# A real-input transform's first step: sums and differences of mirrored rows, five columns of the index grid per product

## The chip, the cores and the metric

One core of a Trainium2 chip. The time is device time of one execution in microseconds (us), lower is better. All runs in this document were in the fast state (granted clock 0.996 to 0.999), so all may be compared. "Before" and "after" are the kernel without and with the change; the variants are named e1 to e10.

## The reference

Eight sequences of 3008 tokens and 256 channels go through a Fourier filter, then all 24064 tokens through a SwiGLU block. Cut to what matters:

```python
x: (8, 3008, 256)   filt_r, filt_i: (1505, 256)   w_gate, w_val: (256, 1536)   w_out: (1536, 256)
X = np.fft.rfft(x, axis=1)
y = np.fft.irfft(X * (filt_r + 1j * filt_i), n=3008, axis=1)
t = y.reshape(24064, 256)
out = (silu(t @ w_gate) * (t @ w_val)) @ w_out
```

## The kernel before

The transform of 3008 = 47 x 64 points is made of short products: the first step transforms along n1 (47 rows, N1) for each of the 64 values of n2. As the input is real, 24 results s (NS), each with a real and an imaginary part, are enough. While TensorE works on the SwiGLU block of batch b, which is the bulk of the time, pieces of the transform of batch b+1 are put between its instructions, by a fixed order (the generators below are advanced at marked places of it). Each `yield` ends a piece. `pin` keeps the order of an engine's instructions as written.

The tables of the first step (both parities h of the row number share one product, so the matrix has two blocks with zeros beside them, 94 by 96):

```python
NR = 2 * N1            # 94
NK = 4 * NS            # 96
NV = 2
N_ONE = 32 // NV       # 16 first steps a batch
...
    w = np.stack([np.cos(ph), -np.sin(ph)], 1)
    wf = np.zeros((N1, 2, NS, 2, 2))
    ...
    for h in range(2):
        wf[:, h, :, :, h] = w.transpose(0, 2, 1)
```

The loads, and the step itself: one product, one copy out of PSUM, one store by ScalarE to a DRAM buffer (d1) that the second step reads back in another order:

```python
            elif u < N_ONE:
                self.x[u] = xpool.tile([NR, NV, C], FP32, name=f"x_{self.b}_{u}", tag="x")
                rows = x[self.b].rearrange("(r n) c -> r n c", n=32)

                for r in (slice(0, 80), slice(80, NR)):
                    self.load(out=self.x[u][r], in_=rows[r, ts(u, NV), :])
...
        def stage1(self, u):

            t1 = t1pool.tile([NK, NV, C], FP32, name=f"t1_{self.b}_{u}", tag="t1", bufs=2)
            ps = self.bank(f"pa_{self.b}_{u}")
            pin(nc.tensor.matmul(out=ps[0:NK], lhsT=wf_t, rhs=self.x.pop(u),
                                         start=True, stop=True))
            self.load_x(u + 2)
            yield
            pin(nc.scalar.copy(out=t1, in_=ps[0:NK]))
            pin(nc.scalar.dma_start(out=self.d1_rows[:, ts(u, NV), :], in_=t1))
```

`self.load` issues on the sync queue; `xpool` has two buffers.

Of the kernel before, what the change touches and what calls it, by code (L numbers as in the profile page):

```python
# [41 lines left out]
FP32 = mybir.dt.float32  # L42
U32 = mybir.dt.uint32
# [5 lines left out]
B, S, C = 8, 3008, 256  # L49
# [4 lines left out]
N1, N2 = 47, 64  # L54
NS, NQ = 24, 64
# [14 lines left out]
NV = 2  # L70
N_ONE = 32 // NV
N_TWO = NS // NV


WO = {1: 0, 7: 1, 2: 2, 3: 3, 5: 4, 6: 5, 4: 6}
# [46 lines left out]
def dft_tables():  # L122
    n1, n2 = np.arange(N1), np.arange(N2)
    s, q = np.arange(NS), np.arange(NQ)
    ph = 2 * np.pi * (np.outer(n1, s) % N1) / N1
    w = np.stack([np.cos(ph), -np.sin(ph)], 1)
    wf = np.zeros((N1, 2, NS, 2, 2))
    wi = np.zeros((NS, 2, 2, N1, 2))

    v = np.stack([2 * np.cos(ph), -2 * np.sin(ph)], 0)  # L130
    v[0, :, 0], v[1, :, 0] = 1.0, 0.0
    for h in range(2):
        wf[:, h, :, :, h] = w.transpose(0, 2, 1)
        wi[:, :, h, :, h] = v.transpose(2, 0, 1) / S
    one = wi[:, :, 0, :, 0].transpose(1, 0, 2).reshape(2 * NS, N1)
    back = np.zeros((128, 10 * N1))
    for tile_, first in zip(BACK, BACK_AT):
        for i, (_, row, a, rows) in enumerate(tile_):
            back[row:row + rows, first + N1 * i:first + N1 * (i + 1)] = one[a:a + rows]


    kap = np.where(q[:, None] < 32, s + N1 * q[:, None], s + N1 * (95 - q[:, None]))
    sg = np.where(q < 32, 1.0, -1.0)[:, None]
    th = 2 * np.pi * ((n2[:, None, None] * kap) % S) / S
    c, sn = np.cos(th), np.sin(th)
    d = np.zeros((2, N2, NS, 2, NQ))
    d[0, :, :, 0] = c.transpose(0, 2, 1)
    d[1, :, :, 0] = sn.transpose(0, 2, 1)
    d[0, :, :, 1] = (-sn * sg).transpose(0, 2, 1)
    d[1, :, :, 1] = (c * sg).transpose(0, 2, 1)  # L150
    d = d.reshape(128, NS, 128)
    de = np.stack([d, d.transpose(2, 1, 0)], 2)

    pairs = np.arange(128).reshape(2, N2).T.ravel()
    later = np.stack([de[:, :, 0], de[:, :, 1][:, :, pairs]], 2)
    f32 = np.float32
    return (wf.reshape(NR, NK).astype(f32), wi.reshape(NK, NR).astype(f32),
            back.astype(f32), np.ascontiguousarray(de).astype(f32),
            np.ascontiguousarray(later).astype(f32))


# [1 line left out]
def kernel(  # L163
# [8 lines left out]
    out: bass.AP,  # L172
):
    nc = tc.nc
    wf_host, wi_host, back_host, de_host, later_host = dft_tables()
    wf_dram = nc.inline_tensor(wf_host, name="wf_tbl")
    wi_dram = nc.inline_tensor(wi_host, name="wi_tbl")
    back_dram = nc.inline_tensor(back_host, name="back_tbl")
    de_dram = nc.inline_tensor(de_host, name="de_tbl").ap()
    later_dram = nc.inline_tensor(later_host, name="later_tbl").ap()  # L180
# [7 lines left out]
    xpool = pool("xp", 2)  # L188
    t1pool = pool("t1", 2)
# [36 lines left out]
    one = cpool.tile([128, 1], FP32)  # L226
# [15 lines left out]
    pin = tc.keep_in_program_order  # L242

    def add(eng, dst, a, b):
        return eng.tensor_tensor(out=dst, in0=a, in1=b, op=ALU.add)  # L245

    def sub(eng, dst, a, b):
        return eng.tensor_tensor(out=dst, in0=a, in1=b, op=ALU.subtract)  # L248
# [221 lines left out]
    preparation = Preparation()  # L470
    TICKS = 20

    back_t = []

    def load_back():

        t = rpool.tile([128, 2, 128, 2], U32, name="back", tag="raw", bufs=2)
        t = t.bitcast(FP32).rearrange("p b f two -> p (b f two)")
        back_t.append(t[:, 0:10 * N1])
        pin(nc.sync.dma_start(out=back_t[0], in_=back_dram.ap()))  # L480
# [6 lines left out]
    def fbank(name):  # L487
        return fps.tile([128, NV, C], FP32, name=name, tag="f")
# [7 lines left out]
    class Spectral:  # L496
# [25 lines left out]
        def load_x(self, u):  # L522
            if self.b == 0:
                rows = x[0].rearrange("(r n) c -> r n c", n=32)
                for a, n in ((0, 4), (4, 4)):
                    for r in (slice(0, 80), slice(80, NR)):
                        self.load(out=x0[u][r, a:a + n, :],
                                  in_=rows[r, 8 * u + a:8 * u + a + n, :])
            elif u < N_ONE:
                self.x[u] = xpool.tile([NR, NV, C], FP32, name=f"x_{self.b}_{u}", tag="x")  # L530
                rows = x[self.b].rearrange("(r n) c -> r n c", n=32)

                for r in (slice(0, 80), slice(80, NR)):
                    self.load(out=self.x[u][r], in_=rows[r, ts(u, NV), :])

        def load_two(self, u):
            if u < N_TWO:
                self.tb[u] = lend("tb", u).rearrange("p i (k c) -> p i k c", k=2)
# [41 lines left out]
        def bank(self, name):  # L580

            if self.b == 0:
                return bank(name).rearrange("p (i c) -> p i c", i=NV)
            return fbank(name)

        def stage1(self, u):

# [21 lines left out]
        def turn(self, u):  # L609

            if u >= N_TWO:
                return
# [9 lines left out]
        def stage2a(self, u):  # L622
# [24 lines left out]
            yield  # L647
            pin(add(nc.vector if self.b == 0 and u == N_TWO - 1 else nc.gpsimd, pt, pt, qt))

        def real_part(self, u):  # L650

            if u < N_TWO and u % 3:
                self.real[u] = early("fr", u)
# [233 lines left out]
    rpool = pool("raw", 1)  # L887
# [11 lines left out]
    with tc.tile_pool(name="start", bufs=1) as spool0:  # L899
# [12 lines left out]
        n = 0  # L912
        while n < NPR - 1:
            pair = ORDER[n][0] in "ABE" and ORDER[n + 1][0] in "ABE"
# [32 lines left out]
        for u in range(N_TWO + lag):  # L947
            if u < N_TWO:
                spec.turn(u + 2)
                step = spec.stage2a(u)  # L950
# [32 lines left out]
        following = Spectral(1)  # L983
# [78 lines left out]
    for b in range(B):  # L1062
        cur, nxt = spec, following if b + 1 < B else None
        spec, following = nxt, Spectral(b + 2)
# [3 lines left out]
            return [s.stage3(k, step) for step in range(4)]  # L1068

        d = [three(cur, k) for k in range(1, NCHUNK)]  # L1070
        one = [nxt.stage1(u) for u in range(N_ONE)] if nxt else []
        two = []
        for u in range(N_TWO + 2) if nxt else ():
            two += [nxt.stage2b(u - 2)] if u > 1 else []
# [21 lines left out]
        for step in range(NCHUNK * NG + (b == B - 1)):  # L1096
            ghost = step == NCHUNK * NG
            k, g = order_of(b)[min(step, NCHUNK * NG - 1)]
            this = None
            pieces = []  # L1100
            if not ghost:
                pieces = plan[step]
                this = Group(b, k, g, cur.y[k], sequence_of(cur, nxt, step))
                if b == 0:
                    preparation.finish(step)
                chunk = {0: 1, 2: 2, 5: 3}.get(step)
                if b and chunk:
                    cur.load_t4(chunk, 0)
            elif before is None:
                break  # L1110
            ends = {ORDER[e - 1]: n for n, (_, e) in enumerate(PIECES)}
            last = ghost or b == B - 1 and step == NCHUNK * NG - 1
            for place, token in enumerate(SCHEDULE):
                if b == 0 and this and place * TICKS % len(SCHEDULE) < TICKS and \
                        (step or place > SCHEDULE.index("A01")):
                    preparation.tick(step)
                old = token.endswith("'")
                op = token.rstrip("'")
                if op[0] == "t":
                    n = int(op[1])  # L1120
                    ps = pieces_before if old else pieces
                    if n < len(ps):
                        next(ps[n], None)
                elif op[0] in "Wo" or op.endswith(".o"):

                    g0 = older if old else before
                    if g0 is not None and (old or not ghost):
                        g0.project(op)
                else:
                    g0 = before if old else this  # L1130
                    if g0 is not None and not (ghost and op[0] == "S"):
                        g0.step(op)
                if old or this is None:
                    continue
                if nxt and (step, op) == ((4, "P2") if b else (5, "A23")):
                    nxt.load_two(0)
                if b + 2 < B and (step, op) == (9, "B01"):
                    for u in range(2):
                        following.load_x(u)
                if b and chunk and op == "B01":  # L1140
                    cur.load_t4(chunk, 1)
                for i in range(2):
                    if nxt and (step, op) == (10, ("A12", "E23")[i] if b else "E23"):
                        nxt.load_t4(0, i)
                for f, args in chores.get((step, op), ()) if b == 0 else ():
                    f(*args)
                if op in ends and not last and (b or step >= NT * NG - 1):
                    reload_weights((g + 1) % NG, ends[op])
            older, before, pieces_before = before, this, pieces
# [33 lines left out]
```

## Time and profile before

| | before |
|---|---|
| median of 3 runs at first, range | 2941.1 us (2937.6 to 2943.2) |
| span of the profiled run | 2935.5 us |
| TensorE, VectorE, ScalarE, GpSimd busy | 99%, 66%, 55%, 54% |
| chain of work that ended last | TensorE 94% |
| first steps: matmul, copy | 112 of each in batches 1 to 7, 0.86 us of TensorE each |

The kernel is bound by TensorE nearly everywhere. So a change pays what it takes off TensorE, less the waits that it gives TensorE. Such waits are short (mostly 0.1 to 1 us) and begin behind other instructions, so the totals by engine hardly show them. What shows them is the chain, the timeline, and a comparison of the two traces matmul by matmul.

### The profile page before, as it was taken

How to read it: one execution, taken by the hardware profiler on the slowest of the kernel's cores; microseconds unless marked ns; L12 is line 12 of the kernel's file. 1: busy time of each engine (PE TensorE's matmuls, PEld its weight loads, DVE VectorE, ACT ScalarE, POOL GpSimd, SP SyncE). 2: the span in 40 equal slices, each digit the busy share in tenths (PEclk: the TensorE clock that was granted, in tenths of full speed). 3: DMA queues.
4: the chain of work that ended last, by engine and by line, in shares of the span. 5: the costliest groups of instructions: out<-in, count | busy, mean ns of one | idle time of the engine just before them, and what ended most of it. 6: DMA issues, size and time to landing. Idle time of an engine off the chain costs nothing.

```text
span 2935.5 us, 57365 instructions
## 1 busy us (share of the span) xinstructions
PE 2901.7 (99%) x20040; PEld 2805.6 (96%) x20040; DVE 1927.4 (66%) x4384; ACT 1609.7 (55%) x4208; POOL 1579.9 (54%) x1759
## 2 busy tenths in 40 slices
PE   7999999999999999999999999999999999999999
PEld 5889999999999999999999999999999999999999
DVE  6888765576655676557765667656666566666665
ACT  6775455555555555555455554555555555555554
POOL 3876655556444655456554556454564545555453
PEclk9999999999999999999999999999999999999999
DMA  8677855575555755556646566556665566644442
GB/s 227 213 258 250 304 189 179 179 229 180 179 182 186 223 186 166 189 183 205 213 155 193 184 203 211 164 177 203 194 199 173 177 208 194 200 139 154 148 130 88
DMA packets 225661, 558.82 MB, mean 190 GB/s; under 512 B 32666, under 2 KB 110474, under 8 KB 225374
## 3 DMA queue, kind: packets, MB, share of 16 engines
q1 hardware_dynamic: 190286, 485.84, 52.6%
q10 hardware_dynamic: 26160, 45.43, 4.3%
q0 software_dynamic: 8928, 23.89, 2.3%
q8 instruction: 161, 2.64, 0.4%
q14 instruction: 126, 1.03, 0.1%
HBM read 459.97 MB, written 95.05 MB: 189 GB/s over the span
## 4 chain that ended last, share of the span: by engine, by line
PE 94%; DVE 1%; POOL 1%; ACT 0%; issue 0%; DVEq 0%; POOLq 0%
PE wa L791 24%; PE wA L870 17%; PE wk L791 16%; PE we L791 12%; PE wG L870 9%; PE wF L870 4%; PE pa L590 3%; PE pd L696 3%; PE pc L662 2%; PE pb L630 2%; PE pd L699 0%; POOL y_t L245 0%; DVE h L838 0%; POOL wt_t L245 0%; POOL wt_t L248 0%
## 5 line engine op out<-in xcount | busy, mean ns | idle before, releaser
L791 PE MATMUL wa<-y_t,wt_t 128*128 128x188 f32 x4464 | 878.8, 323 | 3.8 <-issue 1.4
L791 PEld LDWEIGHTS wa<-y_t,wt_t 128*128 128x128 f32 x4464 | 730.2, 190 | 28.6 <-issue 17.3
L245 POOL TENSOR_TENSOR h<-h 128x376 f32<-128x376 f32 x190 | 182.8, 983 | 779.2 <-DVE h L838 779.2
L870 PE MATMUL wA<-wo_t,h 128*128 128x128 f32 x4608 | 576.9, 275 | 2.3 <-DVE o L245 1.7
L870 PEld LDWEIGHTS wA<-wo_t,h 128*128 128x128 f32 x4608 | 563.0, 192 | 16.3 <-issue 10.8
L791 PE MATMUL wk<-y,wt_t 128*128 128x188 f32 x2976 | 566.2, 323 | 0.0
L248 POOL TENSOR_TENSOR h<-h 128x376 f32<-128x376 f32 x570 | 554.8, 995 | 0.5
L791 PEld LDWEIGHTS wk<-y,wt_t 128*128 128x128 f32 x2976 | 479.1, 190 | 25.9 <-issue 19.8
L248 DVE TENSOR_TENSOR we<-we,m 128x376 f32<-128x376 f32 x576 | 318.4, 556 | 195.2 <-PE we L791 134.1
L791 PE MATMUL we<-y_t,wt_t 128*128 128x188 f32 x2232 | 431.5, 323 | 1.4 <-ACT we L822 1.4
L791 PEld LDWEIGHTS we<-y_t,wt_t 128*128 128x128 f32 x2232 | 369.4, 190 | 1.8 <-ACT we L822 1.7
L248 POOL TENSOR_TENSOR D<-f,f 128x376 f32<-128x376 f32 x288 | 280.7, 988 | 103.3 <-ACT f L806 102.6
L252 DVE SCALAR_TENSOR_TENSOR y<-wk,c 128x376 f32<-128x376 f32 x480 | 244.8, 542 | 131.4 <-ACT we L822 55.0
L826 ACT COPY m<-wa 128x376 f32<-128x376 f32 x576 | 272.0, 472 | 87.1 <-PE wa L791 85.9
L833 ACT ACTIVATE g<-wa 128x188 f32<-128x188 f32 x576 | 187.9, 326 | 187.5 <-PE wa L791 180.0
L870 PE MATMUL wG<-wo_t,h 128*128 128x128 f32 x2304 | 288.3, 275 | 0.6 <-DVE o L245 0.6
L870 PEld LDWEIGHTS wG<-wo_t,h 128*128 128x128 f32 x2304 | 281.4, 192 | 0.8 <-DVE o L245 0.8
L833 ACT ACTIVATE u<-we 128x188 f32<-128x188 f32 x576 | 188.9, 328 | 168.2 <-DVE we L248 149.9
L806 ACT ACTIVATE f<-wk 128x376 f32<-128x376 f32 x288 | 139.4, 484 | 234.4 <-PE wk L791 213.2
L810 ACT COPY c<-wk 128x376 f32<-128x376 f32 x288 | 136.0, 472 | 226.1 <-PE wk L791 226.1
L813 DVE SCALAR_TENSOR_TENSOR x<-wk,f 128x376 f32<-128x376 f32 x192 | 104.3, 543 | 234.4 <-PE wk L791 228.6
L822 ACT COPY we<-y 128x376 f32<-128x376 f32 x480 | 224.1, 487 | 32.9 <-DVE h L838 14.2
(144 smaller groups left out, 3893.8 us busy)
## 6 DMA issues: line engine op xcount, KB each, us to landing
wt_t<-w_all SPq DMA_DIRECT2D x174, 896.0 KB
wt_t<-w_all SPq DMA_DIRECT2D x174, 768.0 KB
d<-t ACTq DMA_DIRECT2D x112, 192.0 KB
lent<-later_tbl SPq DMA_DIRECT2D x84, 256.0 KB
lent<-in_filt_r_dram SPq DMA_DIRECT2D x336, 64.0 KB
lent<-d SPq DMA_DIRECT2D x84, 256.0 KB
d<-lent ACTq DMA_DIRECT2D x84, 256.0 KB
x<-in_x_dram SPq DMA_DIRECT2D x112, 160.0 KB
```

The costliest lines, as they stand in the source:

```text
L245: return eng.tensor_tensor(out=dst, in0=a, in1=b, op=ALU.add)
L248: return eng.tensor_tensor(out=dst, in0=a, in1=b, op=ALU.subtract)
L252: return nc.vector.scalar_tensor_tensor(out=dst, in0=a, scalar=-1.0, in1=b, op0=ALU.mult, op1=ALU.subtract)
L590: pin(nc.tensor.matmul(out=ps[0:NK], lhsT=wf_t, rhs=self.x.pop(u), start=True, stop=True))
L791: pin(nc.tensor.matmul(out=ps[:, z], lhsT=self.wt[:, SLOT[p], z], rhs=rhs, start=start and z == 0, stop=True, skip_group_check=True))
L806: pin(act.mul(self.small(f"f{i}", f"f{i}", 1), t[f"k{i}"], -1.0))
L810: pin(act.copy(out=self.small(f"c{i}", f"c{i}", 1), in_=t[f"k{i}"]))
L813: pin(v.scalar_tensor_tensor(out=dst, in0=t[f"k{j}"], scalar=-1.0, in1=t[f"f{i}" if j == 3 else f"D{at}"], op0=ALU.mult, op1=ALU.add))
L822: pin(act.copy(out=self.bank(f"e{at}"), in_=t[f"y{at}"]))
L826: pin(act.copy(out=self.small(f"m{at}", "m", 4), in_=t[f"a{at}"]))
L833: pin(act.activation(out=self.small(op, "g", 3, 1)[:, 0], in_=ps[:, 1], func=AF.Silu))
L870: pin(nc.tensor.matmul(out=self.tiles[at][:, t, :], lhsT=self.hs[i][:, HID[p], t0:t0 + 128], rhs=wo_t[:, JB * q + i, WO[p], :], start=star ...
```

## The change

In the first step's table, w[n1] holds the factors by which row n1 is multiplied, and w[47 - n1] is the conjugate of w[n1]. So the real part needs only the sums x[n1] + x[47 - n1], the imaginary part only the differences, and each contraction falls from 47 rows to 24 (with row 0) and 23. Then five n2 fit into one product of 120 by 120, and two products with 256 columns each make five n2, where one with 512 columns made four. That is 13 steps a batch for 16. The price: VectorE makes the sums and differences (for step u+1, one piece after step u), and five n2 in one tile make loads and stores of x and of the result a pattern of three dimensions. Batches 2 to 7 are changed; 0 and 1 stay. The diff, with tables and declarations cut:

```diff
@@ dft_tables
+    paired = np.zeros((NP * (NPAIR + 1), 2, NS, NP))          # NP = 5, NPAIR = 23
+    for j in range(NP):
+        paired[NPAIR * j:NPAIR * (j + 1), :, :, j] = w[1:NPAIR + 1]
+        paired[NP * NPAIR + j, 0, :, j] = 1.0
 ... (declarations, and the load of the table once)
@@ load_x
+            elif self.b > 1:
+                if u < N_PAIRED:                              # 13
+                    t = xpool.tile([NP * (NPAIR + 1), 2, C], FP32, name=f"x_{self.b}_{u}", tag="x")
+                    n2, pairs = min(NP * u, N2 - NP), NP * NPAIR
+                    rows = x[self.b].rearrange("(n1 n2) c -> n2 n1 c", n2=N2)
+                    back = bass.AP(tensor=x.tensor,
+                                   offset=x.offset + ((self.b * N1 + N1 - 1) * N2 + n2) * C,
+                                   ap=[[C, NP], [-N2 * C, NPAIR], [1, C]])
+                    self.load(out=t[0:pairs, 0], in_=rows[n2:n2 + NP, 1:NPAIR + 1])
+                    self.load(out=t[0:pairs, 1], in_=back)
+                    self.load(out=t[pairs:pairs + NP, 0], in_=rows[n2:n2 + NP, 0])
+                    self.x[u] = t
@@ stage 1
+        def pair(self, u):
+
+            if u < N_PAIRED:
+                a, b = [self.x[u][0:NP * NPAIR, i] for i in range(2)]
+                pin(sub(nc.vector, differences[u % 2], a, b))
+                pin(add(nc.vector, a, a, b))
+
+        def stage1_paired(self, u):
+
+            t1 = t1pool.tile([NP * NS, 2, C], FP32, name=f"t1_{self.b}_{u}", tag="t1", bufs=2)
+            ps = self.bank(f"pa_{self.b}_{u}")[0:NP * NS]
+            table = paired_t[0]
+            m = NP * NS
+            pin(nc.tensor.matmul(out=ps[:, 0], lhsT=table[:, 0:m], rhs=self.x.pop(u)[:, 0],
+                                 start=True, stop=True))
+            pin(nc.tensor.matmul(out=ps[:, 1], lhsT=table[0:NP * NPAIR, m:2 * m],
+                                 rhs=differences[u % 2], start=True, stop=True))
+            self.load_x(u + 2)
+            yield
+            pin(nc.scalar.copy(out=t1, in_=ps))
+            n2 = min(NP * u, N2 - NP)
+            rows = self.d1.rearrange("(s p) n c -> p s n c", p=2)
+            for i in range(2):
+                pin(nc.scalar.dma_start(out=rows[i, :, n2:n2 + NP], in_=t1[:, i]))
+            yield
+            self.pair(u + 1)
 ... (the first pair of a batch at a place of the previous one; which of the two steps a batch uses)
```

More of the change, by code (lines that the diff above doesn't have):

```diff
@@ L72 @@
 N_TWO = NS // NV
+NP = 5
+NPAIR = N1 // 2
+N_PAIRED = -(-N2 // NP)
 WO = {1: 0, 7: 1, 2: 2, 3: 3, 5: 4, 6: 5, 4: 6}
@@ L152, in dft_tables @@
     de = np.stack([d, d.transpose(2, 1, 0)], 2)
+    paired = np.zeros((NP * (NPAIR + 1), 2, NS, NP))
+    for j in range(NP):
+        paired[NPAIR * j:NPAIR * (j + 1), :, :, j] = w[1:NPAIR + 1]
+        paired[NP * NPAIR + j, 0, :, j] = 1.0
+    paired = paired.reshape(NP * (NPAIR + 1), -1)
     pairs = np.arange(128).reshape(2, N2).T.ravel()
@@ L157, in dft_tables @@
     return (wf.reshape(NR, NK).astype(f32), wi.reshape(NK, NR).astype(f32),
-            back.astype(f32), np.ascontiguousarray(de).astype(f32),
+            back.astype(f32), paired.astype(f32), np.ascontiguousarray(de).astype(f32),
             np.ascontiguousarray(later).astype(f32))
@@ L174 @@
     nc = tc.nc
-    wf_host, wi_host, back_host, de_host, later_host = dft_tables()
+    wf_host, wi_host, back_host, paired_host, de_host, later_host = dft_tables()
     wf_dram = nc.inline_tensor(wf_host, name="wf_tbl")
     wi_dram = nc.inline_tensor(wi_host, name="wi_tbl")
+    paired_dram = nc.inline_tensor(paired_host, name="paired_tbl")
     back_dram = nc.inline_tensor(back_host, name="back_tbl")
@@ L471 @@
     TICKS = 20
-    back_t = []
+    back_t, paired_t, differences = [], [], []
     def load_back():
+        for n in range(3):
+            t = rpool.tile([128, 2, 128], U32, name=f"paired_{n}", tag="pw", bufs=3)
+            t = t.bitcast(FP32).rearrange("p b f -> p (b f)")
+            (differences if n else paired_t).append(t[0:NP * (NPAIR + (not n))])
+        pin(nc.sync.dma_start(out=paired_t[0][:, 0:2 * NP * NS], in_=paired_dram.ap()))
         t = rpool.tile([128, 2, 128, 2], U32, name="back", tag="raw", bufs=2)
@@ L1070 @@
         d = [three(cur, k) for k in range(1, NCHUNK)]
-        one = [nxt.stage1(u) for u in range(N_ONE)] if nxt else []
+        if b:
+            one = [nxt.stage1_paired(u) for u in range(N_PAIRED)] if nxt else []
+        else:
+            one = [nxt.stage1(u) for u in range(N_ONE)]
         two = []
@@ L1139 @@
                         following.load_x(u)
+                if b + 2 < B and (step, op) == (11, "A02"):
+                    following.pair(0)
                 if b and chunk and op == "B01":
```

## The prediction

> **What bounds the kernel now.** I read the page first, part 1 (busy time by engine) and part 4 (the chain that ended last).
>
> ```profile
> PE 2901.7 (99%) x20040; PEld 2805.6 (96%) x20040; DVE 1927.4 (66%) x4384; ACT 1609.7 (55%) x4208; POOL 1579.9 (54%) x1759
> ...
> PE 94%; DVE 1%; POOL 1%; ACT 0%; issue 0%; DVEq 0%; POOLq 0%
> ```
>
> TensorE is busy 99% of the span and holds 94% of the chain. Nothing else is a bound, so time can only be saved by taking TensorE work away, and is lost wherever another engine becomes late enough to make TensorE wait. Next come the groups of instructions, for what the change replaces (`pa` is the transforms' first step):
>
> ```profile
> L590 PE MATMUL pa<-x,wf_t 94*96 94x512 f32 x224 | 114.7, 592 | 0.0
> L594 ACT COPY t<-pa 96x512 f32<-96x512 f32 x112 | 65.1, 581 | 70.4 <-PE pa L590 61.5 <-DMA t<-d 8.8
> ```
>
> 224 records are 112 matmuls, two records for each fp32 one: 16 for each of batches 1 to 7. TensorE never idles before them (0.0). The 592 ns is no cost, because matmuls overlap; the cost is the distance from one start to the next, read from the timeline:
>
> ```profile
> 903.59 1.02 PE L590 MATMUL pa<-x,wf_t 94*96 94x512 f32 x2
> ...
> 904.45 1.28 PE L870 MATMUL wA<-wo_t,h 128*128 128x128 f32 x10
> ...
> 999.74 0.59 PE L630 MATMUL pb<-lent 128*128 128x256 f32 x2
> 1000.18 0.80 PE L791 MATMUL wk<-y,wt_t 128*128 128x188 f32 x4
> ```
>
> A 512-column matmul holds TensorE for 904.45 - 903.59 = 0.86 us, with only 94 rows of contraction and 96 of output. A 256-column matmul with all 128 by 128 takes 1000.18 - 999.74 = 0.44 us. Columns are paid for, rows are not. Last, the waits of the sync queue and of ScalarE:
>
> ```profile
> SPq L511 <- PE pa L590: 271.7, 98, 6.5
> ...
> ACT t L594 <- DMA t<-d: 8.8, 8, 1.7
> ```
>
> The loads of x are issued as soon as TensorE frees their buffer, and ScalarE already stops a little at the first step for a DMA (8 times, up to 1.7 us).
>
> **What the Trainium skill says.** "TensorE: Matmul & The Clock Gate", section "Step-by-step: what each phase is for": throughput follows the moving operand's columns. The timeline agrees (0.86 against 0.44 us). The same page, "LDWEIGHTS (loading the stationary operand)": a weight load costs by its columns, not by its contraction dimension. This trace agrees: 190 ns for 128 columns, 164 ns for 96. "SBUF — State Buffer", section "Who interferes with whom": a VectorE instruction with two SBUF inputs contends with GpSimd instructions that read SBUF. The new sums and differences are of that kind. The trace has such 128x376 operations at 543 ns and 128x256 ones in the preparation at 727 ns, so it does not contradict it. "DMA: Bandwidth & Descriptors", section "Why a DMA increments its semaphore by 16 and not by 1": a queue's DMA is spread over the largest k up to 16 that divides the slowest dimension of both sides, and only k engines post a completion. The trace agrees: that rule makes 32,352 completions of the kernel before, and the trace holds 32,353 packets of 4 bytes.
>
> **The change, part by part.** Batches 2 to 7 change; their first steps run during batches 1 to 6.
>
> 1. TensorE. Removed: 6 x 16 x 0.86 = 82.6 us. Added: 64 n2 at five each make 13 steps of two 256-column matmuls, so 6 x 13 x 2 x 0.43 = 67.1 us. (A 512-column matmul's 0.86 halved is 0.43; `pb` shows 0.44.) This is on the bound, so **15.5 us** are saved. The larger contraction (120, 115) and output (120) cost nothing: 190 ns weight loads stay behind 215 ns of streaming a record.
>
> 2. VectorE. Added: 78 pairs of a subtraction and an addition, 115x256. From 345 ns at 188 columns and 543 at 376, 256 columns take some 0.42 us; with GpSimd in the way, 0.73. That is 0.85 to 1.45 us a pair, 66 to 113 us in all, on an engine busy 1,927 of 2,935. Idle time takes it in total; locally I followed the order of instructions. A pair stands 2 to 3.8 us ahead of its matmul, and in the trace VectorE has finished what stands before it early enough to leave 1.2 to 3.1 us after 0.85 us of work. TensorE should not wait for the sums. What follows on VectorE is late by up to 1 us; its own users need it 1.3 to 2.7 us later at most places, and 0.75 us later at one (u = 9). I count about 0.2 us lost a batch.
>
> 3. ScalarE. 13 copies for 16 (0.58 us each), but two DMA issues (0.31 us each) for one: 13 x 1.20 = 15.6 against 16 x 0.89 = 14.2 us a batch. The busy time hardly moves; an issue more at a tight place costs 0.1 to 0.2 us.
>
> 4. DMA. Bytes stay (3.0 MB a batch each way), in 1 KB pieces for 2 KB ones: 46 ns each in the trace, against 84. More important is the spread. A load's DRAM side now begins with a dimension of 5 and its SBUF side with 115, so k = 5 by the rule: 23 packets on each of five engines. The loads of one step put 47 x 46 ns = 2.2 us on those five engines, where 94 x 84/16 = 0.5 us lay on all. With u = 6 to 12 following each other every 6 us, these five also carry stores and weights (DMA share 0.55 to 0.61 before; I estimate 0.9 and above for the five). A load landed 2.4 us after issue in the median and 5.9 at most; I expect 4 to 7.
>
> 5. Waits by completion counters. In the built program a queue DMA reuses one of eight counters in turn and so waits for the DMA eight before it. One step now issues five DMAs for three, so eight back is nearer. From TensorE's times in the trace: ScalarE's stores of step u = 8 come only 3.8 us after the issue of the loads whose counters they reuse, and one of u = 6 comes 5.1 us after a weight reload (landing 4.6 us in the median, up to 7.7). Against 5 to 6 us of landing, ScalarE stops some 1 to 2 us at u = 8, and up to 1 us at u = 6. Its users leave about 1 us there. So 0.3 to 1.5 us of TensorE a batch are lost.
>
> Sum: -15.5, and 6 x (0.2 + 0.15 + 0.6) = +6 us for parts 2, 3 and 5 together, so about -10 us: 2941 - 10 = **2931 us**.
>
> **Rivals.** (a) All of the gain arrives: every new wait stays within slack. For it: VectorE idles 34%, and 1.2 us or more are left ahead of every matmul. Against it: the 3.8 us. It would be 2,925 us. (b) The DMA becomes the bound of the first step: five engines with 2.2 us a step fall behind, VectorE waits for x with everything else of the feed-forward part behind it, and weight reloads land late because their last share is on the same five. The pair's wait for x comes 7.0 us after the issue at the tightest place (u = 2, 8), and nine at most others; a landing beyond 7 us would be needed often. At 5 us lost a batch this gives 30 us, and 2,955 us. (c) VectorE and GpSimd block each other: GpSimd's operations (0.98 us) hold up the pairs and are held up by them, and pairs take 1.5 to 2 us. GpSimd has several microseconds of slack at most places (its longest waits are for VectorE, 779 us), so I give this 0.05 us a pair, some 4 us.
>
> **Range and chances.** The low end is rival (a) with the luck of the fastest run, about 2,920; the high end is losses that cancel the gain, 2,946. The largest possible gain is 0.5%, so faster by 2% (2,882 us) can't come from this; slower by 2% (3,000 us) would need 75 us of stalls, or nearly 1 us at each of 78 steps. That is possible if VectorE waits for x at each, so 3%.
>
> **What would show it.** Part 1: TensorE busy falls by about 15 us, and the starts of the two new matmuls lie 0.43 us apart. Part 2: 156 new VectorE operations of 0.42 to 0.75 us, and no long wait of TensorE for them. Part 4: loads of x that land later, and 4-byte packets down to about 30,990. Part 5: new waits of ScalarE's first-step rows (store, or what follows it) for DMAs, most at u = 8. The prediction is wrong if VectorE's sums wait for loads of x by more than a microsecond at many steps, if weight matmuls wait for reloads, or if TensorE's idle time grows by more than 15 us from any cause I haven't named.

## The result

After the change the median is **2967.5 us** (2966.9 to 2973.7, 4 runs) against 2940.0 us (2937.6 to 2943.2, 4 runs): 27.5 us slower, outside the predicted range. The ratio is 1.010, interval 1.0085 to 1.0115. A ratio here is the mean time of one kernel's fast runs over that of the other's of the same rounds, so it is not quite the ratio of the medians quoted. By class it is "within 2%", as was said.

The page of the kernel after, busy time by engine and the chain that ended last, the latter by engine and by line:

```profile
PE 2906.6 (98%) x20160; PEld 2833.5 (96%) x20160; DVE 2027.1 (68%) x4540; ACT 1596.5 (54%) x4190; POOL 1595.4 (54%) x1759
...
PE 87%; DMA 3%; ACTq 2%; ACT 2%; DVE 1%; issue 1%; POOL 1%; SPq 0%; DVEq 0%; POOLq 0%
PE wa L846 23%; PE wA L925 15%; PE wk L846 15%; PE we L846 12%; PE wG L925 8%; PE wF L925 4%; PE pd L751 3%; PE pb L685 2%; PE pc L717 2%; ACTq L637 2%; PE pa L627 1%; PE pa L629 1%; DMA wt_t<-w_all 1%; DMA x<-in_x_dram 1%; ACT t L633 1%
```

TensorE has fallen from 94% to 87% of the chain. A new member is ACTq L637, the issue of the first step's stores. VectorE's 100 us more of work (1927 to 2027) were expected. TensorE's busy time did not fall, although its work did: the records overlap (below, records of 0.60 us whose starts lie 0.43 us apart), so a short wait can hide under one. The Trainium skill, "Perfetto Trace Analysis", section "Identifying the Most-Contended Engine", says that matmul busy time is no good measure of how near a kernel is to its limit, as matmuls are pipelined. This trace agrees, and shows the same for comparing two versions.

So I matched every matmul of the two traces in program order and compared the distances between their starts. The saving is there: 96 matmuls of 0.86 us have given way to 156 of 0.43, which makes 15.5 us. The losses, in batches 2 to 7, at places of more than 0.03 us:

| TensorE starts later at | waits for | us in all |
|---|---|---|
| the first step's own matmuls (u = 6, 9, 10, 11) | VectorE's sum and difference | 18.0 |
| wk (12.9), wa (10.4) and we (2.5), the SwiGLU block's matmuls | a ScalarE copy | 25.8 |
| sum | | 43.8 |

The steps u = 6, 9, 10 and 11 lose 0.80, 0.23, 0.98 and 0.99 us in each of the six batches, and no other step loses any. 43.8 - 15.5 = 28.3 us; the spans differ by 2965.3 - 2935.5 = 29.8. Of the 1.5 us left, 1.1 arise before the first changed step starts (at 449.7 us), where TensorE's work is the same in both, and 0.4 are shifts of less than 0.03 us.

**Where ScalarE is late.** First the kernel before around one first step, then the same place after. The columns of a timeline are start, duration, engine, line, operation, names, shapes and count, and in brackets the idle time ahead of it with its releaser:

```profile
1166.67 0.58 ACT L594 COPY t<-pa 96x512 f32<-96x512 f32 x1 [1.65 <-PE pa L590]
1167.29 0.33 ACTq L595 DMA_DIRECT2D d<-t  x1
...
1167.71 0.48 ACT L806 ACTIVATE f<-wk 128x376 f32<-128x376 f32 x1 [0.46 <-POOL h L248]
```

```profile
1176.73 0.60 PE L627 MATMUL pa<-x,paired 120*120 120x256 f32 x2
...
1177.16 0.60 PE L629 MATMUL pa<-paired,paired 115*120 115x256 f32 x2
...
1177.60 1.44 PE L846 MATMUL wk<-y,wt_t 128*128 128x188 f32 x8
1177.80 0.58 ACT L633 COPY t<-pa 120x512 f32<-120x512 f32 x1 [1.66 <-PE pa L629]
1178.41 1.56 ACTq L637 DMA_DIRECT2D d<-t  x2
...
1180.07 0.48 ACT L861 ACTIVATE f<-wk 128x376 f32<-128x376 f32 x1 [1.69 <-DMA d<-t]
...
1180.61 1.54 PE L846 MATMUL wk<-y,wt_t 128*128 128x188 f32 x8 [0.24 <-ACT f L861]
```

The matmuls behave as planned: 1177.16 - 1176.73 = 0.43 us and 1177.60 - 1177.16 = 0.44 us. But the two stores hold ScalarE's queue for 1.56 us, where the one store before held it for 0.33. The copy f starts 0.1 us after the second issue ends, and TensorE's wk waits for f. The profile names f's releaser "DMA d<-t". It is the issue, not the landing: the instructions of the store's line show it (columns: shortest, median and longest ns), first before, then after with who waited (us in all, times):

```profile
L595 ACTq DMA_DIRECT2D d<-t x112: 310/311/356, 103.8 to 2357.5; - x112
```

```profile
L637 ACTq DMA_DIRECT2D d<-t x156: 747/747/1457, 451.3 to 2372.6; - x156
L637 ACTq EVENT_SEMAPHORE  x78: 17/17/38, 450.7 to 2372.6; - x78
...
  ACT f L861: 27.0, 16
  ACT we L877: 23.2, 12
  ACT u L888: 10.1, 6
```

An issue takes 747 ns for 311, and there are two for one. The waits for semaphores ahead of them are 17 to 38 ns long: no store waited for an earlier DMA's completion.

**Where the sums are late.** The groups of the new VectorE instructions, and the timeline at step u = 6:

```profile
L256 DVE TENSOR_TENSOR x<-x 115x256 f32<-115x256 f32 x78 | 67.4, 864 | 2.7
L259 DVE TENSOR_TENSOR paired<-x 115x256 f32<-115x256 f32 x78 | 46.8, 600 | 0.0
```

```profile
1236.49 2.10 POOL L256 TENSOR_TENSOR h<-h 128x376 f32<-128x376 f32 x2 [17.00 <-DVE h L893]
...
1237.05 0.70 DVE L259 TENSOR_TENSOR paired<-x 115x256 f32<-115x256 f32 x1
...
1237.79 1.09 DVE L256 TENSOR_TENSOR x<-x 115x256 f32<-115x256 f32 x1
1238.56 2.13 POOL L259 TENSOR_TENSOR h<-h 128x376 f32<-128x376 f32 x2
...
1238.98 0.66 PE L627 MATMUL pa<-x,paired 120*120 120x256 f32 x2 [0.55 <-issue]
```

The pair takes 1.46 us in the mean (864 + 600) and 1.83 us here, and the matmul starts 0.10 us after its end (1237.79 + 1.09 = 1238.88). Its wait is labelled "issue", which here stands for the late pair. The single instructions have two kinds of duration. The 54 that overlap no GpSimd instruction take 421 ns in the mean, the 102 that overlap one take 897; each of the 78 longer than 650 ns overlaps one. VectorE had no wait for a load of x: it never idled ahead of the differences, which read x first (0.0), and the 2.7 us ahead of the sums have no releaser.

Step u = 9 is different. Its pair is not long (0.88 us in each of the six batches); it starts late, because VectorE itself waited for ScalarE behind the stores of u = 8. The same place in the trace, with both:

```profile
1254.29 1.74 ACTq L637 DMA_DIRECT2D d<-t  x2
...
1256.07 0.88 ACT L877 COPY we<-y 128x376 f32<-128x376 f32 x2 [2.44 <-DMA d<-t]
1256.58 1.01 DVE L263 SCALAR_TENSOR_TENSOR y<-wk,c 128x376 f32<-128x376 f32 x2 [2.56 <-ACT we L877]
...
1257.97 0.42 DVE L259 TENSOR_TENSOR paired<-x 115x256 f32<-115x256 f32 x1
...
1258.42 0.42 DVE L256 TENSOR_TENSOR x<-x 115x256 f32<-115x256 f32 x1
...
1258.94 0.66 PE L627 MATMUL pa<-x,paired 120*120 120x256 f32 x2
```

So the 1.4 us of u = 9 (6 x 0.23) belong to the stores, and 16.6 of the 18.0 us to long pairs.

### The profile page after: what moved, and what is told of

It is laid out like the page before. It is cut to its first block, busy times and chain, and to the rows that moved or that the text cites. A ratio compares the mean times of both kernels' runs of the same rounds, so it can differ in the third digit from the quotient of the medians.

```text
span 2965.3 us, 57854 instructions
## 1 busy us (share of the span) xinstructions
PE 2906.6 (98%) x20160; PEld 2833.5 (96%) x20160; DVE 2027.1 (68%) x4540; ACT 1596.5 (54%) x4190; POOL 1595.4 (54%) x1759
## 4 chain that ended last, share of the span: by engine, by line
PE 87%; DMA 3%; ACTq 2%; ACT 2%; DVE 1%; issue 1%; POOL 1%; SPq 0%; DVEq 0%; POOLq 0%
PE wa L846 23%; PE wA L925 15%; PE wk L846 15%; PE we L846 12%; PE wG L925 8%; PE wF L925 4%; PE pd L751 3%; PE pb L685 2%; PE pc L717 2%; ACTq L637 2%; PE pa L627 1%; PE pa L629 1%; DMA wt_t<-w_all 1%; DMA x<-in_x_dram 1%; ACT t L633 1%
## 5 line engine op out<-in xcount | busy, mean ns | idle before, releaser
L256 POOL TENSOR_TENSOR h<-h 128x376 f32<-128x376 f32 x190 | 185.1, 995 | 772.1 <-DVE h L893 762.5
L259 POOL TENSOR_TENSOR h<-h 128x376 f32<-128x376 f32 x570 | 566.6, 1015 | 0.5
```

The source lines that it names most:

```text
L256: return eng.tensor_tensor(out=dst, in0=a, in1=b, op=ALU.add)
L259: return eng.tensor_tensor(out=dst, in0=a, in1=b, op=ALU.subtract)
```

## The experiments

The theories after this reading:

- **A**: the two stores, each with a DRAM side of three dimensions, hold ScalarE in the issue itself.
- **B**: VectorE's sums and differences are blocked by GpSimd and come too late for their places.
- **C** (the prediction's rival (b)): loads over five DMA engines land late, and all else follows from it.

Each variant is the changed kernel with one edit unless said otherwise. Three rounds each, five for e9 and e10. "Loss" is TensorE's, matched as above in the profiled runs against the trace of the kernel before; "other" is what it loses at other places (mostly wA and wF, which read what VectorE makes). The reference time is that of the kernel before in the same rounds.

| | median us | before us | ratio, interval | loss: sums | loss: ScalarE | other |
|---|---|---|---|---|---|---|
| after | 2967.5 | 2940.0 | 1.0100 (1.0085 to 1.0115) | 18.0 | 25.8 | |
| e1 stores on sync queue | 2945.0 | 2937.4 | 1.0025 (1.0010 to 1.0040) | 19.6 | 0 | |
| e2 pairs earlier | 2959.9 | 2937.4 | 1.0069 (1.0054 to 1.0084) | 0 | 27.4 | 1.7 |
| e3 both | 2929.6 | 2937.4 | 0.9971 (0.9957 to 0.9986) | 0 | 0 | 4.9 |
| e4 before, two stores | 2963.3 | 2937.4 | 1.0090 (1.0073 to 1.0107) | | 23.7 | |
| e5 flat store | 2946.9 | 2937.9 | 1.0031 (1.0016 to 1.0046) | 23.0 | 0 | |
| e6 loads over 15 engines * | 2965.6 | 2937.9 | 1.0094 (1.0077 to 1.0111) | 17.7 | 25.0 | |
| e7 e1, operand from PSUM * | 2924.5 | 2937.9 | 0.9956 (0.9942 to 0.9971) | 0 | 0 | 0 |
| e8 e3, loads over 15 engines * | 2926.8 | 2937.9 | 0.9962 (0.9947 to 0.9977) | 0 | 0 | 1.8 |
| e9 before, stores on sync queue | 2938.0 | 2938.3 | 1.0010 (0.9996 to 1.0023) | | | |
| e10 e3, flat store | 2927.5 | 2938.3 | 0.9964 (0.9952 to 0.9977) | 0 | 0 | 2.2 |

\* wrong result on purpose. In every row that was matched, the span before, less 15.5 us (not for e4), plus the loss, comes to within 1 to 5 us of the variant's span. Nearly all of this rest (1.1 to 4.6 us) arises in the first 445 us, before the first changed step; shifts too small for the matching make 0.5 us at most.

### e1: stores on the sync queue

```diff
-                pin(nc.scalar.dma_start(out=rows[i, :, n2:n2 + NP], in_=t1[:, i]))
+                pin(nc.sync.dma_start(out=rows[i, :, n2:n2 + NP], in_=t1[:, i]))
```

> The changed kernel with its first-step stores issued by the sync queue in place of ScalarE; nothing else moves. In the changed kernel's trace a store's issue holds ScalarE for 747 ns, two a step, where the kernel before had one of 311 ns, and TensorE then waits for ScalarE's f, wa and we copies. Comparing the two traces matmul by matmul, 4.4 us of the 7.4 us lost per batch lie at such places. Theory A (issue time on ScalarE): these 4.4 us a batch go, 6 x 4.4 = 27 us, so 2941 us; TensorE's waits at the first step's own matmuls (3.0 us a batch) stay. Theory C (the loads on five DMA engines and late landings are what costs): loads and stores still run on the same few engines, so within 5 us of 2967.

Measured 2945.0 us, 4 us above theory A's figure: the waits for sums grew by 1.6 us, and the first 445 us took 3.4 us longer than in the trace of the changed kernel. All waits for ScalarE's copies are gone; the waits for sums stay at three steps (u = 6 and 11: 1.19 us each a batch, u = 10: 0.88). The one at u = 9 is gone with the stores, as said above. The issues are as long on the sync queue (773 ns in the median), but nothing in TensorE's way stands behind them there.

### e2: each pair one piece earlier

```diff
                 pin(nc.scalar.dma_start(out=rows[i, :, n2:n2 + NP], in_=t1[:, i]))
-            yield
             self.pair(u + 1)
+            yield
```

> The changed kernel with each pair of sum and difference asked for one slot sooner (right after the previous step's store instead of one slot later). Theory B (VectorE's pairs take 1.46 us in the mean, up to 2.5, because each waits for a GpSimd operation to end, and so come too late for their matmul at u = 6, 9, 10 and 11): the 3.0 us a batch of waits at those matmuls go, 18 us, so about 2949 us. Theory C: the pair comes sooner, so its loads of x have not landed yet (4.6 us in the median, 6.9 at most, against some 7 us from issue to pair now and less than 6 then); VectorE waits for x and the time rises over 2967.

Measured 2959.9 us in the median, where theory B said about 2949; the profiled run was the fastest, 2953.6. In its trace TensorE no longer waits for sums, and its waits for ScalarE stay. What made the other three runs 6 us longer was not traced. VectorE now does wait for x. In the group of the differences (the last column is idle time and what ended it):

```profile
L259 DVE TENSOR_TENSOR paired<-x 115x256 f32<-115x256 f32 x78 | 47.2, 605 | 22.6 <-DMA x<-in_x_dram 22.5
L627 PE MATMUL pa<-x,paired 120*120 120x256 f32 x156 | 46.6, 379 | 0.0
```

### e3: both

The edits of e1 and e2 together.

> Both edits together. Theories A and B together: all of the 45 us lost is gone and the 15.5 us of TensorE time saved are left, so about 2924 us, faster than the kernel before (2940). If they overlap (one wait hides the other), somewhere between 2924 and 2940.

Measured 2929.6 us, faster than before by 0.3%; 4.9 us of other loss keep it above 2924. In the spans of the profiled runs, against the kernel after, e1 gains 20.8 us, e2 13.5 and both 36.9. The parts add up to 2.6 us less than the whole, and each loss grows when the other is taken away alone: 19.6 us at the sums for 18.0, and 27.4 at ScalarE for 25.8, together 3.2. (By medians the parts lack more, since e2's is 6 us above its profiled run.) The page's chain for e3:

```profile
PE 57%; DVE 0%; DMA 0%; issue 0%; SPq 0%; DVEq 0%
```

The walk back along this chain stops at 1236.6 us, so it covers the last 58% of the span only, and the 57% is not to be compared with the 87% and 94% above. In that part TensorE holds nearly all of it, and ScalarE and its queue are gone.

### e4: the kernel before with two stores in three dimensions

The other direction: the change's store in the kernel that has none of the rest of it. The table's columns are permuted so that the result stays right.

```diff
-            pin(nc.scalar.dma_start(out=self.d1_rows[:, ts(u, NV), :], in_=t1))
+            rows = self.d1_rows.rearrange("(z s) n c -> s z n c", z=4)
+            for i in range(NV):
+                pin(nc.scalar.dma_start(out=rows[:, :, NV * u + i], in_=t1[:, i]))
```

> The kernel before, its matmuls and loads untouched; only the store of a first step of batches 2 to 7 is issued as two DMAs, whose DRAM side is 24 by 4 rows of 1 KB that do not merge (the rows' order is undone in the first step's table, so the result stays right). Theory A: each issue takes some 0.7 us instead of 0.31 once, ScalarE is held for 1.1 us more at each of 96 steps, and the kernel before slows down by 15 to 35 us without any sums or five-engine loads. Theory C: the kernel before does not change (within 3 us), since its loads stay on 14 and 16 engines. If the issue stays at 0.31 us, the number of packets or engines sets it and the run says nothing on A.

Measured 2963.3 us, 26 us slower than before and within theory A's 15 to 35, with TensorE's waits at the same matmuls as after (wk 13.3, wa 10.3 us). The store's line in e4 and who waited for it:

```profile
L603 ACTq DMA_DIRECT2D d<-t x192: 755/756/1356, 451.4 to 2383.2; - x192
...
  ACT we L830: 29.6, 18
  ACT f L814: 29.3, 17
```

So this part alone makes the larger half of the miss, without pairs and without loads over five engines.

### e5: one flat store, still by ScalarE

The table's columns are put in the order (n2, s), so that a step's result is one piece of DRAM: 120 rows of 2 KB. The second step's loads and table follow it; the result stays right.

```diff
-            rows = self.d1.rearrange("(s p) n c -> p s n c", p=2)
-            for i in range(2):
-                pin(nc.scalar.dma_start(out=rows[i, :, n2:n2 + NP], in_=t1[:, i]))
+            pin(nc.scalar.dma_start(out=self.d1_flat[NS * n2:NS * (n2 + NP)],
+                                    in_=t1.rearrange("q i c -> q (i c)")))
```

> The changed kernel with only the first step's store laid out anew: the table's columns in the order (n2, s), so that what one step of five n2 stores is one piece of 120 rows of 2 KB, one DMA in two dimensions, still issued by ScalarE; the second step reads it back from that layout (two loads for one, a permuted table; the result stays right). Theory A (ScalarE is held by the issue of two stores whose DRAM side has three dimensions, 0.75 us each): the issue falls to one of about 0.33 us, TensorE's 25.8 us of waits for ScalarE's f, wa and we copies go, and the waits for the sums (18 to 20 us) stay: 2945 us, +-4, as where the stores were moved to the sync queue. Rival A' (what costs is that the store sits in ScalarE's order and waits there for a completion counter, whatever its shape): no change, 2960 to 2968.

Measured 2946.9 us, as e1, and no wait for ScalarE is left:

```profile
L647 ACTq DMA_DIRECT2D d<-t x78: 322/323/572, 452.2 to 2351.6; - x78
```

The issue of 120 rows takes 323 ns flat, and took 747 as a pattern of 24 by 5 by 256 with the same 120 rows. So the layout costs, not the number of rows, nor that ScalarE issues it. Rival A' had no change; it falls. (The loss at the sums is 23.0 us for 19.6 in e1, some of it at u = 1, 7 and 12; why was not looked into.)

Three dimensions alone are not what makes an issue long. The second step reads the buffer d back by a load of three dimensions, 2 by 128 rows of 1 KB, and its issue on the sync queue is short already in the kernel before:

```profile
L511 SPq DMA_DIRECT2D lent<-d x84: 388/389/1565, 259.5 to 2533.0; - x84
```

The change's loads of x, 5 by 23 rows, hold the same queue for 752 ns in the median. Which part of the pattern costs stays open.

### e6: loads of x over 15 engines (wrong result on purpose)

Nearly the same bytes (240 KB a step for 235) in the same number of DMAs and partitions, as plain rows of 2 KB (the two lines that set `rows` and `at` are left out):

```diff
-                    self.load(out=t[0:pairs, 0], in_=rows[n2:n2 + NP, 1:NPAIR + 1])
-                    self.load(out=t[0:pairs, 1], in_=back)
-                    self.load(out=t[pairs:pairs + NP, 0], in_=rows[n2:n2 + NP, 0])
+                    for a, n in ((0, 45), (45, 45), (90, 30)):
+                        self.load(out=t[a:a + n].rearrange("q i c -> q (i c)"),
+                                  in_=rows[at + a:at + a + n])
```

> The changed kernel, with its loads of x over 15 engines (wrong result on purpose: the same bytes of x, the same 120 partitions, three DMAs a step, but plain rows of 2 KB). Theories A and B: the landing falls from 4.6 us to about 2.5, and nothing is gained by it, since VectorE waits for x only 2.7 us in all: 2967, +-4. Theory C (five engines and late landings are what costs, my rival (b)): a fall of 15 us or more, to below 2952.

Measured 2965.6 us: nothing gained. Loads landed 2.7 us after issue in the median, for 4.6 after the change. Theory C falls as a cause of the miss.

### e7: the second operand from PSUM (wrong result on purpose)

e1, with the second operand of sums and differences read from the bank of the step before (`self.ps`, kept by a line left out here). Everything else, GpSimd's work too, stays where it is.

```diff
                 a, b = [self.x[u][0:NP * NPAIR, i] for i in range(2)]
+                if u:
+                    b = self.ps[0:NP * NPAIR, 1]
```

> The changed kernel with its stores on the sync queue, and the second operand of every sum and difference after a batch's first read from PSUM in place of SBUF (wrong result on purpose). Theory B (a VectorE instruction with two SBUF inputs is blocked by a GpSimd instruction that reads SBUF): the sums and differences take their free time, 0.42 to 0.5 us each, in place of 0.73 on average, the waits of TensorE for them (19.6 us) go or fall under 5 us, and the time is 2925 to 2930. Rival: the pair is late for its place in VectorE's order, not for its length, or is blocked whatever it reads: 2945, +-3.

Measured 2924.5 us, 0.5 us below the band; the loss is zero. The groups:

```profile
L256 DVE TENSOR_TENSOR x<-x,pa 115x256 f32<-115x256 f32 x72 | 30.3, 421 | 2.5
L259 DVE TENSOR_TENSOR paired<-x,pa 115x256 f32<-115x256 f32 x72 | 29.7, 413 | 0.0
```

In e1 the same groups took 868 and 712 ns. The pair at u = 6, in e1 and in e7:

```profile
1229.64 1.92 POOL L256 TENSOR_TENSOR h<-h 128x376 f32<-128x376 f32 x2 [15.91 <-DVE h L893]
...
1230.66 1.18 DVE L259 TENSOR_TENSOR paired<-x 115x256 f32<-115x256 f32 x1
...
1231.88 1.10 DVE L256 TENSOR_TENSOR x<-x 115x256 f32<-115x256 f32 x1
...
1233.08 0.66 PE L627 MATMUL pa<-x,paired 120*120 120x256 f32 x2 [0.96 <-issue]
```

```profile
1221.16 1.93 POOL L256 TENSOR_TENSOR h<-h 128x376 f32<-128x376 f32 x2 [16.20 <-DVE h L895]
...
1222.18 0.41 DVE L259 TENSOR_TENSOR paired<-x,pa 115x256 f32<-115x256 f32 x1
...
1222.63 0.42 DVE L256 TENSOR_TENSOR x<-x,pa 115x256 f32<-115x256 f32 x1
...
1223.49 0.60 PE L629 MATMUL pa<-x,paired 120*120 120x256 f32 x2
```

The GpSimd pair begins some 1.0 us ahead of the difference in both. In e1 the difference ends 0.28 us after GpSimd (1231.84 against 1231.56), in e7 it passes through. The matmul comes 2.42 us after the pair's start in e1 and 1.31 in e7: 1.11 us between them, close to the loss of 1.19 at this step. It also gives the room that the change has there: 1.31 us for 0.87 us of unblocked pair, so 0.4 us. It is as tight at u = 10 and 11, the other two places of long pairs.

### e8: e3 with loads over 15 engines (wrong result on purpose)

> The kernel with stores on the sync queue and each pair one piece earlier (2929.6 us before), with loads of x over 15 engines (wrong result on purpose, as in the other). There VectorE waits for x 18.2 us in all. If late landings are what is left of the loss (theory C as the next cause), these waits fall under 4 us and the time to 2925, +-2; if the 4.9 us left are the longer pairs on VectorE, it stays at 2929.6, +-2.

Measured 2926.8 us, inside the band of theory C (2923 to 2927) and 0.8 us below that of the other theory, but with an interval that overlaps e3's. The trace is clearer: VectorE's waits for x went from 18.2 us in e3 to 0.1, and the loss from 4.9 to 1.8. So theory C is a small limit behind the other two, about 3 us by the matching.

### e9: the kernel before with stores on the sync queue

> The kernel before with the first step's stores of batches 2 to 7 on the sync queue and nothing else changed. It is the fair base for the mended kernel. ScalarE waits before these copies for a DMA only 8.8 us in all, and TensorE loses nothing there in the kernel before. Theory: no change, within 2 us of the kernel before. Rival (the sync queue alone makes the mended kernel faster, not the new products): a fall of 6 us or more, so that the mended kernel's gain of 8 us is not the change's.

Measured 2938.0 against 2938.3 us: no change. With its flat short store, the kernel before has nothing to gain from the move, so the comparison of e3 and e10 with the kernel before is fair.

### e10: e3 with the flat store

> The best version that the runs point to: the change with stores on the sync queue, each pair one piece earlier, and the store flat (120 rows of 2 KB, one DMA, two dimensions; the result stays right). The sync queue then issues one short store for two long ones, so that loads of x are issued sooner behind it. With the pairs early, VectorE waited 18.2 us for x; with loads over 15 engines these waits were gone and the time 2926.8 (wrong result). Theory (part of this wait is the sync queue's issue): VectorE's waits for x fall below 12 us and the time to 2928, +-1.5. Rival (the landing over five engines alone): 2929.6, +-1, waits of 16 us or more.

Measured 2927.5 us, the fastest version with a right result: 0.36% faster than before. VectorE's waits for x, in e3 and in e10:

```profile
L259 DVE TENSOR_TENSOR paired<-x 115x256 f32<-115x256 f32 x78 | 46.5, 597 | 18.2 <-DMA x<-in_x_dram 18.2
```

```profile
L261 DVE TENSOR_TENSOR paired<-x 115x256 f32<-115x256 f32 x78 | 46.2, 592 | 12.7 <-DMA x<-in_x_dram 12.7
```

They fell, but to 12.7 and not below 12, and the ratio (0.9964) lies within the interval of e3's (0.9971). That e10 is faster than e3 is likely, not shown.

## Why the prediction was wrong

By its own steps:

1. **TensorE's saving was right.** Distances of 0.43 and 0.44 us, 15.5 us in all. (One reading under it was loose: 190 ns for 128 columns and 164 for 96 compare loads that differ in rows too. The trace after separates them: 183 ns for 120 columns, with 120 rows and with 115.) The sign that it named, TensorE's busy time down by 15 us, did not come (2901.7 to 2906.6); that sum cannot show it.
2. **VectorE: "TensorE should not wait for the sums" failed: 18.0 us.** The durations were nearly foreseen: 0.85 to 1.45 us a pair, 1.46 measured. But the room was compared with the unblocked 0.85 us alone, while the same paragraph had the blocked one. 16.6 us come from pairs of 1.8 us and more at u = 6, 10 and 11; a mean hides the two kinds. The room was mis-sized too: "1.2 to 3.1 us" were to be left after 0.85 us of work, and e7 shows 0.4 us at these three steps. e7 shows that the length of the pairs makes these waits. The other 1.4 us (u = 9) are a short pair that starts late behind the stores of part 3.
3. **ScalarE: "two DMA issues (0.31 us each)" failed: 25.8 us.** The 0.31 us belongs to a flat store of 96 rows. The new store's pattern takes 0.75 us, so 1.49 us a step for the assumed 0.62. The step's further error was "0.1 to 0.2 us" for an issue more: behind the first step stand copies that TensorE waits for (f, wa, we). In its sum this was 6 x 0.15 = 0.9 us; with the 1.4 us of u = 9 the runs show 27.2. ScalarE's busy time (1609.7 to 1596.5) gave no warning, for it leaves issues out. e4 and e5 show this step from both sides.
4. **DMA: right, and without effect on the result.** The spread over five engines is confirmed (30,994 packets of 4 bytes, 30,990 predicted), landings too (4.6 us in the median, 6.9 at most, for 4 to 7). e6 shows that nothing of the miss comes from it.
5. **Completion counters: this mechanism did not show.** The waits of ScalarE's rows for "DMA" look like its confirmation: the rows after the stores of u = 8 have the most, 10.8 us (those of u = 6, foreseen too, have 8, but so have 8 to 10 us those of u = 0, 2, 3 and 4, which were not foreseen). They were the issues themselves: semaphore waits ahead of the stores took 38 ns at most, and e5, which stores through the same counters in one flat DMA, is free of the waits.

Of the rivals, (a) is what the change gives when its two side effects are taken away: 2924.5 us in e7 with a wrong result, 2925 predicted. (b) is refuted by e6 as the bound, and is worth some 3 us behind the rest (e8). (c) named the right mechanism for the sums and mis-sized it at 4 us: it counted total time and GpSimd's slack, where TensorE's slack at three places a batch decided. And no rival asked whether the price of an issue depends on the pattern.

What stays open: how the issue time depends on the pattern. Of patterns of three dimensions, stores of 24 by 5 and 24 by 4 rows of 1 KB took 747 and 756 ns and loads of 5 by 23 rows 752, but a load of 2 by 128 rows 389; two flat stores took 311 and 323, and the flat store also reads whole rows of its tile. No run varied one part of a pattern alone. Open too is why the first 445 us differ by 1 to 5 us between the traces.

## What to carry to other kernels

When a change alters the access pattern of a DMA, take the issue's duration from a DMA of the new pattern, not from the one that it replaces, and ask which instruction stands behind it on the issuing engine; a queue with nothing urgent behind it is the place for a slow issue, or a layout that makes it flat. When an engine's new work may be blocked, compare the blocked duration, not the free one or the mean, with the room at the tightest place. And do not judge a kernel with a full engine by that engine's busy total: match the two traces instruction by instruction.

## What the Trainium skill lacked or had wrong

- "DMA: Bandwidth & Descriptors", section "Anatomy of one DMA — SWDGE (gpsimd) path", calls descriptor generation "small, variable". That is the GpSimd path; no page that I read gives how long a DMA holds ScalarE's or the sync engine's queue by its pattern. Here a flat store held ScalarE 311 to 323 ns and one of 24 by 5 or 24 by 4 rows 747 to 756 ns, which cost TensorE 25.8 us after the change; a load of 2 by 128 rows held the sync queue 389 ns. "Perfetto Trace Analysis", section "DMA Instruction — HWDGE (DVE, Sync)", says that the profiled interval includes waiting for the descriptor generator's lock, generation and the push of the semaphore. The trace agrees that the engine is held through it; the lock does not explain the 747 ns, since the 25 of the changed kernel's stores that overlapped no issue of the sync queue took 747 ns in the median too.
- "SBUF — State Buffer", section "Who interferes with whom", is right that two SBUF inputs contend with GpSimd's reads and one does not (e7: 413 to 421 ns for 712 to 868 in e1). It gives no duration for it: in the kernel after, 421 ns free, 897 in the mean when overlapping, 1486 at most (1891 in e1), at 115x256 fp32.
- "Perfetto Trace Analysis", section "Identifying the Most-Contended Engine", advises the share of peak FLOPs and LDWEIGHTS busy time in place of matmul busy time for judging how near a kernel is to its limit. It does not say how to compare two versions, and for that neither busy time served: with 15.5 us less work both rose (matmul 2901.7 to 2906.6 us, LDWEIGHTS 2805.6 to 2833.5), the second because there are 60 matmuls more, narrower ones, and so more loads of weights.
